# An FNet mixing layer plus a GEGLU layer on one core: the first token tile and the pass borders in a new order, a pool of their own for tiles that transfers empty, the sums of a and b made earlier, and adding transfers into the output

## Chip, cores and metric

The kernel runs on one core of a Trainium2 chip. The metric is the device time of one execution in microseconds (us). The kernel before took 836.38 us, the median of three runs (831.19 to 836.46).

## What is computed

```python
xn = layernorm(x)                                   # x: 2048 tokens x 512, fp32
a = einsum("sd,ed->se", xn, dft_hid_re)             # 512 x 512 matrices
b = einsum("sd,ed->se", xn, dft_hid_im)
y = einsum("ts,se->te", dft_seq_re, a) - einsum("ts,se->te", dft_seq_im, b)   # 2048 x 2048
h = gelu(xn @ w_gate) * (xn @ w_up)                 # 512 -> 1792
out = x + y + h @ w_down
```

## The kernel before, in words

**Arithmetic.** Every fp32 operand of TensorE is split in two: ACT writes the rounded high part (`split_hi`, line 67), DVE subtracts it for the low part (`split_lo`, line 70). A product (`mm3`, line 81) is three multiplications of 128 x 512: high by high, and the two mixed ones. Each large product is made as seven block products (numbered 0 to 6) of sums and differences of blocks; DVE makes the sums. So PE waits for low parts (psl, wl, xT..l) on DVE and for high parts (psh, wh, xT..h) on ACT. All engines work through their instructions in the order in which the program issues them (`manual_schedule`).

**First stage.** Eight token tiles of 128 tokens (`TILES`, t0 to t7) are loaded, normalized, transposed on PE (tile pt), copied (xq), split into xT0 to xT6, and multiplied with the 512 x 512 matrices (d, split into wph and wpl); `plain_out` sends the results to the DRAM tensor ab, which holds a and b for each of the 16 token tiles.

**Units.** 28 units (`unit`, 14 for each half of the tokens; NP is 14). A unit makes the seven products for gate (even) or up (odd) into the PSUM tiles a, b, c; the ACT copies from a and b (lines 568, 575, 580) stand between them. Its other work (weight splits, sums, splits of h) stands in a list with costs (`background`), worked off at four places of the unit by `run(share)`; what is left is put into `carry` for the next unit. Down projections (`down`, PSUM tiles dn) fill in between: ACT copies dn into a tile part, and POOL issues a transfer that adds it to the DRAM tensor partial (lines 443 to 447). In units 4 to 11 DVE also normalizes the transposed second half of x (`norm_xr`).

**Spectral stage.** Between unit 13 and 14 a and b of the second token half are made by seven products in PSUM tiles sa and sb (`spectral`, `prepare`), and go to ab.

**Passes.** Four passes of 16 steps (`steps`) contract over the 16 token tiles. Pass 0 and 1 make, for the two column halves, the products 0, 6, 2; pass 2 and 3 make 5, 4, 3, 1. A step takes three (or four) panels of the sequence matrices (pan, 256 KB each, loaded by SP), sums them on DVE (`sum_step`), splits them into psh and psl (`split_step`), and multiplies with a0, s34 (pass 0, 1) or with b (bth, btl) and qr (qrhl) of the token tile (`contract`). In pass 0 each step also loads a and b of a tile (`load_ab`), makes four half-tile sums of them on DVE (`side_sums`: w34 and qr) and splits some (`side_split`); b is loaded again by SP and split with qr in pass 1 (`late_side`). The PSUM banks of a pass are first filled from partial by ACT (`seed`, line 693). At the end of a pass `drain` empties them: in pass 0 and 1 into tiles tot, from which six transfers add to partial, and, after subtracting from the residual x (xres), into the DRAM tensor ends by four plain transfers; in pass 2 and 3 into the output.

**Memory and queues.** Almost every 128 x 512 tile comes from one pool `mem` of 67 slots (`slot`), pairs of tiles from `big` (21). A tile that a transfer empties (part, tot, xres, ab, xr) sits in its slot until that transfer has landed; who gets the slot next waits for it. SP issues the plain loads in program order, POOL the stores to ab, partial and ends.

Of the kernel before, what the change touches and what calls it, by code (L numbers as in the profile page):

```python
# [27 lines left out]
BIG = 21  # L28
SLOTS = 67
# [5 lines left out]
def fnet_geglu_kernel(ctx: ExitStack, tc: tile.TileContext, x, xt, cs, dh, wgu, wd, out):  # L35
# [8 lines left out]
    mem = ctx.enter_context(tc.tile_pool(name="mem", bufs=SLOTS))  # L44
    small = ctx.enter_context(tc.tile_pool(name="small", bufs=4))
# [4 lines left out]
    def slot(name, dtype=F32, shape=(P, D)):  # L50
        return mem.tile(list(shape), dtype, name=name, tag="mem")

# [41 lines left out]
    ends = dram.tile([2, 2, 2, P, CH], F32, name="ends")  # L94
    ab = dram.tile([NS, 2, P, D], F32, name="ab")
    xnt = dram.tile([2, ND, P, CH], F32, name="xnt")
# [120 lines left out]
    def plain_out(n, m):  # L217
        t = slot("ab")
        nc.scalar.activation(t, xps.pop((n, m)), AF.Copy, scale=-1.0 if m else 1.0)
        to_ab(n, m, t)  # L220
# [7 lines left out]
    def spectral(sp, k, i):  # L228
# [9 lines left out]
        elif k == 1:  # L238
            t = slot("a")
            nc.scalar.activation(t, sa[i], AF.Copy)  # L240
            to_ab(n, 0, t)
        elif k == 5:
            s5[i] = slot("s5")
            nc.scalar.activation(s5[i], sb[i], AF.Copy)
        elif k == 6:
            s6[i] = slot("s6")
# [3 lines left out]
        elif k == 3:  # L250
            t = slot("b")
            nc.scalar.activation(t, sb[i], AF.Copy, scale=-1.0)
            to_ab(n, 1, t)
        elif k == 2:
            nc.vector.tensor_add(s5[i], sa[i], s5[i])
            to_ab(n + TPC, 0, s5[i])
# [24 lines left out]
    def norm_xr(h, t, j):  # L281
        v = xr[h, t, j]
        nc.vector.tensor_sub(v, v, xst[t, 0])
        nc.vector.tensor_mul(v, v, xst[t, 1])
        nc.gpsimd.dma_start(xnt[t, 2 * h + j], v)
# [51 lines left out]
    def prepare(k):  # L337
        for j in range(2):
            sum_x(k, j)
            sum_w(k, j)  # L340
            split(*x1_split(k, j))
# [91 lines left out]
    def down(qs, r, js):  # L433
# [6 lines left out]
        def add():  # L440
            for j in js:
                t = slot("part")
# [7 lines left out]
    SPLIT_AHEAD, SUM_AHEAD, LOAD_AHEAD = 1, 2, 3  # L450
# [8 lines left out]

    FILL = {0: 2, 1: 2, 2: 2, 3: 2, 4: 2, 5: 1}  # L460

    def background(n):
        work = []

# [23 lines left out]
        else:  # L488
            for k in range(4):
# [8 lines left out]
        if n == 2 * NP - 2:  # L498
            put(sum_step, 0)
            put(side_sums, 0, cost=4)  # L500
            put(side_split, 0, cost=3)
        if n == 2 * NP - 1:
            put(split_step, 0, cost=6)
            put(sum_step, 1)
            put(side_sums, 1, cost=4)
# [5 lines left out]
    def unit(n):  # L511
# [4 lines left out]
        if n == 2 * NP - 3:  # L516
            load_ab(0)
            load_step(0)
        if n == 2 * NP - 2:
            for r in GROUP[0]:  # L520
                load_acc(0, r)
            load_ab(1)
            load_step(1)
        if n == 2 * NP - 1:
            load_step(2)
            load_ab(2)
# [42 lines left out]
        multiply(4, c, True)  # L569
        while carry:  # L570
# [19 lines left out]
        if n == 0:  # L590
            add_w(1)
            split_w(1)
        run(.75)
# [3 lines left out]
        d3()  # L597
        high(n, (1, 1))
        low(n, (0, 0))
        nc.vector.tensor_add(q6, c, q6)  # L600
        if n % 2 == 1:
# [6 lines left out]
    GROUP = {0: (0, 6, 2), 1: (5, 4, 3, 1)}  # L608
    passes = [(0, 0), (1, 0), (0, 1), (1, 1)]
    steps = [(c, g, n) for c, g in passes for n in range(NS)]  # L610
    pan, pan_src, pan_hl = {}, {}, {}

# [20 lines left out]
    def split_step(i):  # L633
        if i < len(steps):
            src = pan_src.pop(i)
            for r in GROUP[steps[i][1]]:
                pan_hl[i, r] = hl_tile("ps")
# [4 lines left out]
    def load_ab(n):  # L642
        if n < NS:
            t = pair("abr", F32)
            for m, v in enumerate((av, bv)):
                v[n] = t[:, m]
                nc.sync.dma_start(v[n], ab[n, m])

    def load_b(n):
        bv[n] = slot("b")  # L650
        nc.sync.dma_start(bv[n], ab[n, 1])

    def side_sums(n):
        if n < NS:
            v, w = qr[n], w34[n] = slot("qr"), slot("w34")
            ah, bh = ([t[:, :HD], t[:, HD:]] for t in (av[n], bv.pop(n)))
            nc.vector.tensor_sub(w[:, :HD], ah[0], ah[1])
            nc.vector.tensor_sub(v[:, :HD], bh[1], ah[1])
            neg_sub(v[:, HD:], v[:, :HD], ah[0])
            neg_sub(w[:, HD:], v[:, HD:], bh[0])  # L660

    def side_split(n):
        if n < NS:
            t = pair("s34")
            a0[n], s34[n] = hl_half("a0"), (t[:, 0], t[:, 1])
            split(a0[n], av.pop(n)[:, :HD])
            split(s34[n], w34.pop(n))

# [13 lines left out]
    acc, bank, late = {}, {}, {}  # L682

    def load_acc(c, r):
        t = pair("acc", F32)
        for j in range(2):
            acc[c, r, j] = t[:, j]
            nc.sync.dma_start(acc[c, r, j], partial[c, r, j])
# [6 lines left out]
    def load_residual(c):  # L695
        for h in range(2):
            for j in range(2):
                late[c, h, j] = slot("xres")
                nc.sync.dma_start(late[c, h, j], xt[c, 1, 2 * h + j])

    def load_ends(c):
        for h in range(2):
            for j in range(2):
                late[c, h, j] = slot("ends")
                nc.sync.dma_start(late[c, h, j], ends[c, h, j])

    def store(c, h, j, t, src):
        nc.sync.dma_start(out[2 * h + j, 2 * c + t], src)
# [3 lines left out]
    def drain(c, r, j):  # L712
        ps = bank.pop((c, r, j))
        if r in (0, 6):
            t = slot("tot")
            nc.scalar.activation(t, ps, AF.Copy)
            for u in (5, 1) if r == 0 else (3,):
                nc.gpsimd.dma_start(partial[c, u, j], t, accum_op=OP.add)  # L718
        if r in (6, 2):
            t = late.pop((c, int(r == 6), j))  # L720
            nc.vector.tensor_sub(t, ps, t)
            nc.gpsimd.dma_start(ends[c, int(r == 6), j], t)
        if r == 5:
            us[j] = slot("u")
            nc.scalar.activation(us[j], ps, AF.Copy)
        if r == 4:
            v = slot("v")
            nc.vector.tensor_add(v, ps, us[j])
            for h in range(2):
                t = late.pop((c, h, j))  # L730
                neg_sub(t, v, t)
# [230 lines left out]
```

## Time and profile before

| what | value |
| --- | --- |
| median of three runs | 836.38 us (831.19 to 836.46) |
| the profiled execution's own time | 834.16 us |
| its span, first to last instruction | 832.3 us |
| mean granted TensorE clock | 0.993 |
| PE, DVE, ACT, POOL busy | 97%, 83%, 61%, 16% of the span |
| transfers | 170.65 MB, mean 205 GB/s |

| stretch (us from the span's start) | what runs |
| --- | --- |
| 0 to 55 | first stage |
| 55 to 246 | units 0 to 13 |
| 246 to 286 | spectral stage |
| 286 to 489 | units 14 to 27 |
| 489 to 578 | pass 0 |
| 578 to 650 | pass 1 |
| 650 to 740 | pass 2 |
| 740 to 832 | pass 3 |

How to read it: a row of the timeline has start and duration in us, engine, line, operation, output and inputs, shape and count, and in brackets the idle time of that engine just before and what ended it. `<-DMA partial<-tot` means that a transfer's landing ended the wait. "issue" means that the profile shows nothing that was waited for. A row of the table by stretches has, for each engine, busy us and the number of instructions, then the granted clock, the share of time for which the 16 DMA engines were busy, and GB/s. Some records of multiplications are missing (3514 are there).

### The profile page before, as it was taken

What the parts mean: (1) busy time and instruction counts of PE and PEld (TensorE: products, weight loads), DVE (VectorE), ACT (ScalarE), POOL (GpSimd) and SP (SyncE); (2) the same over time, 40 slices, a digit from 0 to 9 for tenths busy, and PEclk for the clock granted to TensorE, in tenths of its full rate; (3) what the DMA queues carried; (4) which work ended last, traced back from release to release, by engine and by line L of the source; (5) the groups of instructions that cost most, each with busy time, mean ns of one, the idle gap of its engine ahead of it and who ended that gap; (6) DMA issues with size and microseconds to landing.
All of it is one profiled execution on the core that took longest, in us unless ns stands there. A gap on an engine that the chain in (4) does not pass through costs nothing.

```text
span 832.3 us, 11558 instructions
## 1 busy us (share of the span) xinstructions
PE 808.4 (97%) x3514; PEld 656.6 (79%) x3514; DVE 693.5 (83%) x1292; ACT 509.2 (61%) x976; POOL 133.0 (16%) x186
## 2 busy tenths in 40 slices
PE   7999999999999999999999989999899899999998
PEld 4878887788887888888888768788688678887886
DVE  6777999789889758778887979998798699879992
ACT  4566776576686466586666585657566564364441
POOL 0310112222221322132222211112200300000000
PEclk8999999999999999999999999999999999999999
DMA  9722636877891466676577979999998987788732
GB/s 332 274 102 88 184 121 141 198 146 151 238 227 52 177 99 124 133 204 104 109 143 179 230 200 264 278 322 350 317 309 296 318 283 219 236 287 311 252 102 101
DMA packets 88446, 170.65 MB, mean 205 GB/s; under 512 B 10416, under 2 KB 10944, under 8 KB 88256
## 3 DMA queue, kind: packets, MB, share of 16 engines
q1 hardware_dynamic: 67424, 122.46, 44.0%
q0 software_dynamic: 20672, 47.20, 28.1%
q8 instruction: 27, 0.44, 0.2%
q14 instruction: 35, 0.29, 0.1%
q10 hardware_dynamic: 288, 0.26, 0.1%
HBM read 120.59 MB, written 51.39 MB: 207 GB/s over the span
## 4 chain that ended last, share of the span: by engine, by line
PE 43%; issue 31%; DVE 9%; POOL 9%; DMA 5%; ACT 3%; SPq 0%; POOLq 0%; DVEq 0%; ACTq 0%
PE m L81 29%; POOL partial L447 6%; PE b L81 3%; PE dn L81 3%; PE xp L81 3%; PE a L81 2%; DMA partial<-part 2%; DVE psl L70 2%; PE c L81 2%; PE sa L81 1%; DMA partial<-tot 1%; POOL partial L445 1%; POOL partial L718 1%; DMA acc<-partial 1%; DMA pan<-in_cs 1%
## 5 line engine op out<-in xcount | busy, mean ns | idle before, releaser
L67 ACT ACTIVATE psh<-pan 128x512 fp32r<-128x512 f32 x224 | 127.2, 623 | 94.9 <-PE m L81 40.7
L70 DVE TENSOR_TENSOR psl<-pan,psh 128x512 fp32r<-128x512 f32 x224 | 141.1, 685 | 14.1 <-DMA partial<-tot 7.5
L447 POOL DMA_DIRECT2D partial<-part x92 | 80.1, 883 | 264.7 <-ACT part L443 255.4
L443 ACT ACTIVATE part<-dn 128x512 f32<-128x512 f32 x112 | 66.4, 603 | 37.3 <-PE dn L81 30.3
L81 PE MATMUL m<-psh,s 128*128 128x512 f32 x256 | 84.9, 393 | 0.0
L81 PE MATMUL m<-psh,qrhl 128*128 128x512 f32 x256 | 84.2, 390 | 0.5 <-ACT psh L67 0.5
L70 DVE TENSOR_TENSOR wl<-ws,wh 128x512 fp32r<-128x512 f32 x84 | 55.3, 685 | 2.3 <-ACT wh L67 1.6
L81 PEld LDWEIGHTS m<-psh,s 128*128 128x128 f32 x256 | 48.7, 190 | 10.2
L81 PEld LDWEIGHTS m<-psh,qrhl 128*128 128x128 f32 x256 | 48.0, 188 | 10.7 <-ACT psh L67 0.9
L81 PE MATMUL m<-psl,qrhl 128*128 128x512 f32 x128 | 50.5, 395 | 2.4 <-DVE psl L70 2.4
L81 PE MATMUL m<-psl,s 128*128 128x512 f32 x128 | 50.4, 394 | 1.4 <-DVE psl L70 1.4
L67 ACT ACTIVATE wh<-ws 128x512 fp32r<-128x512 f32 x84 | 49.6, 628 | 1.6 <-DMA partial<-part 1.6
L81 PE MATMUL m<-psh,bth 128*128 128x512 f32 x128 | 49.9, 390 | 0.0
L81 PE MATMUL m<-psh,btl 128*128 128x512 f32 x128 | 49.8, 389 | 0.0
L81 PE MATMUL m<-psl,bth 128*128 128x512 f32 x128 | 49.8, 389 | 0.0
L81 PE MATMUL m<-psh,a 128*128 128x512 f32 x128 | 45.4, 395 | 3.5 <-ACT psh L67 1.4
L583 DVE TENSOR_TENSOR w<-c,w 128x512 f32<-128x512 f32 x28 | 19.4, 691 | 34.5 <-ACT w L580 34.2
L580 ACT ACTIVATE w<-b 128x512 f32<-128x512 f32 x28 | 16.7, 597 | 39.6 <-PE b L81 38.3
L81 PE MATMUL b<-xT3h,w 128*128 128x512 f32 x112 | 39.3, 392 | 1.2 <-ACT w L580 1.2
L70 DVE TENSOR_TENSOR wl<-wx,wh 128x512 fp32r<-128x512 f32 x28 | 19.2, 687 | 24.8 <-ACT wh L67 19.6
L70 DVE TENSOR_TENSOR htl<-s,hth 128x512 fp32r<-128x512 f32 x56 | 36.1, 686 | 4.5 <-ACT hth L67 4.1
L422 DVE TENSOR_TENSOR s<-s 128x512 f32<-128x512 f32 x56 | 37.4, 688 | 0.9
(275 smaller groups left out, 2181.1 us busy)
## 6 DMA issues: line engine op xcount, KB each, us to landing
pan<-in_cs SPq DMA_DIRECT2D x224, 256.0 KB, 4.4
partial<-part POOLq DMA_DIRECT2D x112, 256.0 KB, 4.5
wx<-in_wgu SPq DMA_DIRECT2D x56, 256.0 KB, 3.9
abr<-ab SPq DMA_DIRECT2D x32, 256.0 KB, 5.6
wd<-in_wd SPq DMA_DIRECT2D x28, 256.0 KB, 3.0
acc<-partial SPq DMA_DIRECT2D x28, 256.0 KB, 6.0
d<-in_dh SPq DMA_DIRECT2D x16, 256.0 KB, 6.1
ab<-ab POOLq DMA_DIRECT2D x16, 256.0 KB, 2.4
```

The costliest lines, as they stand in the source:

```text
L67: nc.scalar.activation(t[0], src, AF.Copy)
L70: nc.vector.tensor_sub(t[1], src, t[0].bitcast(F32))
L81: nc.tensor.matmul(ps, a[u][:, sl], b[v], start=first and r == 0, stop=last and r == 2, skip_group_check=resumed)
L422: nc.vector.tensor_sub(t, u, v)
L443: nc.scalar.activation(t, ps[j], AF.Copy)
L445: nc.gpsimd.dma_start(partial[sp, r, j], t)
L447: nc.gpsimd.dma_start(partial[sp, r, j], t, accum_op=OP.add)
L580: nc.scalar.activation(w, b, AF.Copy)
L583: nc.vector.tensor_add(w, c, w)
L718: nc.gpsimd.dma_start(partial[c, u, j], t, accum_op=OP.add)
```

## The change

It has five parts. The counts of PE's instructions stay the same.

1. First token tile: its high part is split before ACT turns to the second tile; the tile is normalized by one DVE instruction instead of ACT; the matrices are loaded ahead of the third tile, and both products of t0 come before the transposition of t1. For the later tiles ACT's copy xq comes ahead of DVE's low part.
2. A pool `ship` of nine tiles for what transfers empty (ab, a, b, s5, s6, xn, part, tot, neg, u, v, o, and the new sums); `mem` shrinks to 60 slots, `big` to 20.
3. The sums of a and b are made in the units (unit 1 and 14 to 26, one or two tiles each) and stored to a new DRAM tensor sd. Pass 0 loads half of a and one tile of sd instead of a and b; pass 1 loads b and the other tile of sd, both issued by POOL (`load_late`), two steps ahead of use.
4. Pass borders: seeds for products 2 and 6 of pass 0 are made inside unit 27, product 0 isn't seeded (DVE adds its partial sum at the drain); the loads of partial (acc) are issued by POOL; panels are loaded, summed and, from step 3 of pass 0 to the end of pass 1, split one step further ahead; splits and sums at a border are placed between its products. In the spectral stage sums and splits are spread over its four blocks.
5. The residual goes into the output by eight DRAM-to-DRAM copies in the first stage, and the drains add to it by transfers (`out_y`, four per pass in pass 0 and 1, eight in pass 2 and 3 together); the tensor ends with its loads and subtractions is gone.

```diff
+    def ship(name):
+        return out_pool.tile([P, D], F32, name=name, tag="ship")
...
     def norm_xr(h, t, j):
         v = xr[h, t, j]
         nc.vector.tensor_sub(v, v, xst[t, 0])
-        nc.vector.tensor_mul(v, v, xst[t, 1])
-        nc.gpsimd.dma_start(xnt[t, 2 * h + j], v)
+        w = ship("xn")
+        nc.vector.tensor_mul(w, v, xst[t, 1])
+        nc.gpsimd.dma_start(xnt[t, 2 * h + j], w)
...
+    SIDE_UNITS = (1,) + tuple(range(NP, 2 * NP - 1)) + (NP + 2, NP + 4)
...
+        for k in SIDE_AT.get(n, ()):
+            for f in side_sums(k):
+                put(f, cost=1)
...
+        if n == 2 * NP - 1:
+            seed(0, SEEDED[0][0])
...
+    def split_upto(i):
+        return max(i + 1, min(i + 2, 2 * NS)) if i > 2 else i + 1
...
+    def side_sums(n):
+        v, w = ship("qr"), ship("w34")
...
+            for m, t in enumerate((w, v)):
+                nc.gpsimd.dma_start(sd[n, m], t)
...
+    def load_late(n):
+        if n < NS:
+            bv[n], qr[n] = slot("b"), slot("qr")
+            nc.gpsimd.dma_start(bv[n], ab[n, 1])
+            nc.gpsimd.dma_start(qr[n], sd[n, 1])
...
     def drain(c, r, j):
         ps = bank.pop((c, r, j))
         if r in (0, 6):
-            t = slot("tot")
-            nc.scalar.activation(t, ps, AF.Copy)
+            t = ship("tot")
+            if r == 0:
+                nc.vector.tensor_add(t, ps, acc.pop((c, r, j)))
+            else:
+                nc.scalar.activation(t, ps, AF.Copy)
             for u in (5, 1) if r == 0 else (3,):
                 nc.gpsimd.dma_start(partial[c, u, j], t, accum_op=OP.add)
         if r in (6, 2):
-            t = late.pop((c, int(r == 6), j))
-            nc.vector.tensor_sub(t, ps, t)
-            nc.gpsimd.dma_start(ends[c, int(r == 6), j], t)
+            t = ship("neg")
+            if r == 6:
+                nc.vector.tensor_scalar_mul(t, ps, -1.0)
+            else:
+                nc.scalar.activation(t, ps, AF.Copy, scale=-1.0)
+            nc.gpsimd.dma_start(out[2 * int(r == 6) + j, 2 * c + 1], t, accum_op=OP.add)
...
         if r == 4:
-            v = slot("v")
-            nc.vector.tensor_add(v, ps, us[j])
+            v = ship("v")
+            neg_sub(v, ps, us[j])
             for h in range(2):
-                t = late.pop((c, h, j))
-                neg_sub(t, v, t)
-                store(c, h, j, 1, t)
+                nc.gpsimd.dma_start(out[2 * h + j, 2 * c + 1], v, accum_op=OP.add)
...
+    nc.vector.tensor_scalar(xs[t0], xs[t0], stats[:, 0, 0:1], scale[:, 0, 0:1], op0=OP.subtract, op1=OP.mult)
...
+                nc.gpsimd.dma_start(out[2 * h + j, 2 * sp + 1], xt[sp, 1, 2 * h + j])
...
+    late_at = {NS + 2 + k: k for k in range(NS - 4)}
+    late_at.update({2 * NS + 2 * k: NS - 4 + k for k in range(4)})
...
+        if i + 2 in late_at:
+            load_late(late_at[i + 2])
```

The first place is ACT at the start. Before (L110 loads half of t0, L121 is the root, L137 the normalization, L67 a high part, L176 the copy xq; x_114 is t0, x_121 t1, d are the matrices):

```order
L110 DMA x_114<-in_x 128x256
L121 ACT_TABLE_LOAD
L121 ACTIVATE w<-stats,eps 128x1
L137 ACTIVATE x_114<-x_114,scale 128x512
L121 ACTIVATE w<-stats,eps 128x1
L67 ACTIVATE wph<-d_119 128x512
L67 ACTIVATE xT0h<-pt 128x2x128
```

Now (lines have moved by five: L126 is the root, L72 a high part):

```order
L115 DMA x_117<-in_x 128x256
L126 ACT_TABLE_LOAD
L126 ACTIVATE w<-stats,eps 128x1
L72 ACTIVATE xT0h<-pt 128x2x128
L72 ACTIVATE xT1h<-pt 128x2x128
L72 ACTIVATE wph<-d_126 128x512
L72 ACTIVATE wph<-d_128 128x512
```

The high part of t0 stands four instructions further ahead: the normalization, the second tile's root and one split no longer stand before it.

The second place is POOL at the border from pass 0 to pass 1. Before:

```order
L447 DMA partial<-part 128x512 x44
L718 DMA partial<-tot 128x512 x5
L722 DMA ends<-xres 128x512
L718 DMA partial<-tot 128x512
L722 DMA ends<-xres 128x512 x3
L718 DMA partial<-tot 128x512 x5
```

Now (L455 adds part, L747 tot to partial, L754 adds to the output, L704 loads b, L705 loads qr):

```order
L455 DMA partial<-part 128x512
L747 DMA partial<-tot 128x512 x5
L754 DMA out_y<-neg 128x512
L747 DMA partial<-tot 128x512
L754 DMA out_y<-neg 128x512 x3
L704 DMA b<-ab 128x512
L705 DMA qr<-sd 128x512
L704 DMA b<-ab 128x512
L705 DMA qr<-sd 128x512
```

Six adding and four plain transfers have become ten adding ones, and the loads of b and qr, which SP issued or which weren't there, now stand behind them.

The third place is ACT at the same border. Before (L716 empties a bank into tot, L693 seeds one):

```order
L716 ACTIVATE tot<-m 128x512 x2
L693 ACTIVATE m<-acc 128x512 x2
L67 ACTIVATE psh<-pan 128x512 x3
L67 ACTIVATE bth<-b 128x512
L67 ACTIVATE qrhl<-qr 128x512
L67 ACTIVATE psh<-pan 128x512 x3
```

Now (L745 and L753 empty banks, L72 makes high parts):

```order
L745 ACTIVATE tot<-m 128x512 x2
L753 ACTIVATE neg<-m 128x512 x2
L72 ACTIVATE psh<-pan 128x512 x9
L72 ACTIVATE bth<-b 128x512
L72 ACTIVATE qrhl<-qr 128x512
L72 ACTIVATE psh<-pan 128x512 x3
```

The first split of b stands behind nine panel splits instead of three. These nine are for steps 18, 19 and 20; the three behind qrhl are for step 21 (pass 1 begins with step 16).

## The prediction on record

> **What bounds the kernel now.** I read the page's head first, then the waits of PE, then the stretches, then the timelines where those waits lie.
>
> ```profile
> span 832.3 us, 11558 instructions
> ...
> PE 808.4 (97%) x3514; PEld 656.6 (79%) x3514; DVE 693.5 (83%) x1292; ACT 509.2 (61%) x976; POOL 133.0 (16%) x186
> ```
>
> PE is the bound and does the same multiplications after the change. So only what is not PE's work can be won: 832.3 less 808.4 is 24 us, and some half-clock time inside the 808. Where that lies, PE's waits say (total us, times, longest):
>
> ```profile
> PE m L81 <- DVE psl L70: 5.5, 5, 2.0
> PE xp L81 <- ACT xT0h L67: 2.3, 1, 2.3
> PE sa L81 <- ACT a L240: 1.9, 1, 1.9
> PE m L81 <- ACT psh L67: 1.8, 2, 1.4
> PE b L81 <- ACT b L568: 1.7, 1, 1.7
> ...
> PE b L81 <- ACT w L580: 1.2, 2, 1.0
> PE m L81 <- ACT m L693: 1.1, 1, 1.1
> PE m L81 <- DVE a L70: 1.0, 1, 1.0
> PE c L81 <- ACT xT4h L67: 0.5, 1, 0.5
> ...
> PE c L81 <- DVE w L583: 0.5, 1, 0.5
> PE dn L81 <- DVE htl L70: 0.3, 1, 0.3
> ```
>
> These are 17.8 us in 18 stops. Each stop also costs about 0.25: the first multiplication behind one has a row of 0.50 where the pipelined ones have 0.39 (below), and the pitch behind it is wider. The stretches (PE, PEld, DVE, ACT, POOL busy; clock; DMA share; GB/s):
>
> ```profile
> 9.28:17.44 8.16, 7.68 (x21) 5.15 (x22) 6.21 (x18) 3.98 (x10) 0.00 (x0) 0.63 1.05 392
> 286.20:489.00 202.80, 201.11 (x887) 166.02 (x885) 155.41 (x294) 132.24 (x258) 46.70 (x58) 1.00 0.69 150
> 589.00:599.25 10.25, 6.48 (x19) 4.54 (x19) 7.69 (x13) 7.01 (x14) 1.68 (x3) 0.83 1.06 334
> 602.00:632.00 30.00, 30.00 (x134) 24.86 (x133) 29.97 (x51) 20.51 (x39) 0.00 (x0) 1.00 0.88 295
> ```
>
> In the units (row 2) PE is full and DVE at 77%. At the border of pass 0 and 1 (row 3) the clock falls to 0.83 over 10.25 us: 1.7 us lost beside the stops.
>
> **The change, part by part**, against the profiled execution's own 834.16 us (2.2 below the median of 836.38, inside the runs' 831.19 to 836.46).
>
> *1. Start.*
>
> ```profile
> 4.28 0.43 DVE L206 CAST wph<-d 128x512 fp32r<-128x512 f32 x1
> 5.03 0.16 DVE L128 SCALAR_TENSOR_TENSOR scale<-w 128x1 f32<-128x1 f32 x1
> 6.33 0.63 PE L151 MATMUL pt<-ident,x 128*128 128x128 f32 x4 [0.51 <-issue]
> 8.87 0.36 ACT L67 ACTIVATE xT0h<-pt 128x256 fp32r<-128x256 f32 x1
> 9.28 0.80 PE L81 MATMUL xp<-wph,xT0h 128*128 128x512 f32 x1 [2.32 <-ACT xT0h L67]
> ```
>
> The transposes of t0 end at 6.96, but its high part starts at 8.87, since ACT has other work ahead. Now: scale ready 5.19; one DVE normalization, priced as the DVE cast of the same size, 0.43; transposes 0.63; high part 0.36; three handovers of some 0.07: first product at 6.8, or −2.5, of which I give back 0.2 because products then wait for t1's columns. −2.3. Bounds: −1.5 if the second matrix is not there before 7.8; −4 if the half-clock time at the start also shrinks. The xT4h stop (0.5) falls to the new order of xq and low parts: −0.5 (0 to −0.75).
>
> The Trainium skill ("TensorE: Matmul & The Clock Gate", Part 1, what the clock gate does) has PE at half rate until about 3.4 us of sustained work. The row 9.28:17.44 has 0.63 over 8.16, a loss of 3.0; by that rule it would be 1.7, and the time 1.3 lower; I keep the row's.
>
> *2. The ship pool.*
>
> ```profile
> 154.71 0.69 DVE L70 TENSOR_TENSOR wl<-wx,wh 128x512 fp32r<-128x512 f32 x1 [4.03 <-DMA partial<-part]
> ...
> 589.78 0.69 DVE L70 TENSOR_TENSOR psl<-pan,psh 128x512 fp32r<-128x512 f32 x1 [3.77 <-DMA partial<-tot]
> ...
> 661.84 1.15 ACT L67 ACTIVATE psh<-pan 128x512 fp32r<-128x512 f32 x2 [7.00 <-DMA partial<-tot]
> ...
> partial<-part POOLq DMA_DIRECT2D x112, 256.0 KB, 4.5
> ...
> b<-ab SPq DMA_DIRECT2D x16, 256.0 KB, 4.3
> ```
>
> Splits stood still because a slot still held a tile that was leaving. With tiles that leave in a pool of their own this wait goes to whoever makes the next such tile. In the units part's transfer lands 4.5 us after issue, and nine tiles cover that; so the ACT w stops (1.2 in 2) go with their 2 × 0.25: −1.7 (bounds 0 and −1.7). The DVE w stop stays.
>
> *3. Sums of a and b in units 14 to 26 and unit 1.*
>
> ```profile
> 568.05 0.42 DVE L657 TENSOR_TENSOR w<-abr 128x256 f32<-128x256 f32 x1
> ...
> 478.13 0.63 ACT L67 ACTIVATE s<-w 128x512 fp32r<-128x512 f32 x1 [3.76 <-DVE w L77]
> ```
>
> Four sums of a tile are 4 × 0.4 = 1.6 us; fifteen tiles from unit 14 on make 24 on 155.4 of 202.8: 179, or 88%. PE sees none of it as long as DVE has room: units 4 to 11 carry two more 128x512 operations each, and show one DVE stop of 0.5. I take +1.0 (two such stops with what follows them); bounds 0 and +16 (thirteen units with 1.25 each). The split that waited at 478.13 held up ACT's copy b (1.7 stop): it moves to unit 27; −1.95 and +0.75 back for unit 27's larger list: −1.2. Pass 0 is relieved of 14 × 1.6 on DVE and half of its loads.
>
> *4. Spectral stage:* sums and splits spread over four blocks; the ACT a stop (1.9) goes: −1.9 (0 to −2.3, with its 0.25).
>
> *5. Start of pass 0:* two products seeded in unit 27, the third added at the drain. The m seed (1.1), DVE a (1.0) and htl (0.3) stops and one psl stop of 0.7 go, with 4 × 0.25 but less 0.2 for a longer drain: −3.9 (−1 to −4.1).
>
> *6. Border of pass 0 and 1.* Two things happen. The slot wait of 3.77 goes. But on POOL ten adding transfers now stand ahead of the loads of b and qr, and ACT's split of b stands ahead of the panel split of step 21 (step 36 at the next border).
>
> ```profile
> 575.64 2.64 POOL L718 DMA_DIRECT2D partial<-tot  x3 [6.60 <-ACT tot L716]
> 582.84 0.88 POOL L718 DMA_DIRECT2D partial<-tot  x1 [4.55 <-issue]
> 584.85 0.87 POOL L718 DMA_DIRECT2D partial<-tot  x1 [1.13 <-issue]
> ...
> 586.88 0.85 POOL L718 DMA_DIRECT2D partial<-tot  x1 [0.59 <-issue]
> ...
> 589.96 1.12 POOL L722 DMA_DIRECT2D ends<-xres  x2 [2.23 <-issue]
> 591.83 0.55 POOL L722 DMA_DIRECT2D ends<-xres  x1 [0.74 <-issue]
> ```
>
> Three adding transfers go out at once, the fourth 7.2 later, then one every d; only three seem to be under way at a time. So the tenth goes out at 7.2 + 6d behind the first, and the loads at 7.2 + 7d. They take 0.3 to issue, 4.5 to land (partial's row; b's has 4.3), and 1.1 goes for the two high parts ahead of the panels: ready at 13.1 + 7d. PE's need:
>
> ```profile
> 534.49 4.08 PE m L81 x18
> ...
> 577.84 0.39 PE L81 MATMUL m<-psh,a 128*128 128x512 f32 x1
> ...
> 590.52 0.50 PE L81 MATMUL m<-psl,s 128*128 128x512 f32 x1 [1.41 <-DVE psl L70]
> 594.80 0.50 PE L81 MATMUL m<-psl,a 128*128 128x512 f32 x1 [0.99 <-DVE psl L70]
> ...
> 665.00 0.50 PE L81 MATMUL m<-psl,qrhl 128*128 128x512 f32 x1 [1.97 <-DVE psl L70]
> ```
>
> Step 16 begins 2.2 behind the first adding transfer; step 21 is five steps of 4.08 later, at 22.6. At the other border steps of 24 products take 5.44, so step 36 is at 2.2 + 4 × 5.44 = 24.0. What is d? Over the rows (591.83 − 582.84) / 4 = 2.25, while panels crowd the DMA engines (1.06); the longest interval is 3.1; three under way with 4.5 each, as in the units, give 1.5. Half of what crowds there (a, b and all panels of the next steps) is lighter after the change, so I take the middle, 1.9: ready at 26.4, PE stops 3.8 and 2.4 us. Border 0/1: before, 1.4 + 1.4 + 1.0 + 3 × 0.25 + 1.7 clock = 6.2; after, 3.8 + 0.25 + 1.7 = 5.75; −0.45. Border 1/2: before, 0.5 + 2.0 + 2 × 0.25 = 2.95; after, 2.65 without a loss of clock (none there before either); −0.3. Border 2/3: one psl stop of 0.4 goes, −0.6.
>
> *At nothing:* norm_xr's other target (same count on DVE); the DRAM copies of the residual, under the first stage's products, whose transfers have nobody waiting at once (ab is first read in unit 1); the drains (DVE has four operations per border before and after, ACT loses the seeds of product 0); the end, where adding transfers precede the last plain store and land inside its time (0 to +3).
>
> **Sum:** −2.3 − 0.5 − 1.7 + 1.0 − 1.2 − 1.9 − 3.9 − 0.6 = −11.1, borders −0.75: −11.85. 834.16 − 11.85 = **822.3 us**.
>
> **Rivals.** Without the two borders the sum is 823.06; each case then adds its borders less the 9.15 of before.
> - *The queue is quick* (d 1.5): ready at 23.6, stops 1.0 and 0. 823.06 + 1.25 − 9.15 = 815.2. For it: the units' 4.5. Against: every interval quoted.
> - *The queue is as slow as before* (d 2.25): ready 28.85, stops 6.25 and 4.85, each with 0.25 and 1.7 of clock: 15.0. 828.9. For it: the rows as they stand.
> - *Slower than before:* d is 3.1, since ten adding transfers alternate with panels. Ready 34.8, stops 12.2 and 10.8, with 2 × 1.95: 26.9, so 840.8. It decides from d of 2.6, where the borders' 20.2 eat all of 11.1. Against: one interval alone was that long.
> - *DVE becomes the bound in the units:* 88% is a mean over units with unequal lists, and some come near to full. 13 × 1.25 = 16.2 in place of 1.0: 837.5. For it: pass 1, full at 29.97 of 30, shows how little is left then. Against: units 4 to 11.
> - *Pass 1 is bound by transfers:* a step loads five tiles, not four: share 0.88 × 5/4 = 1.10, so 12 steps × 4.08 × 0.10 = 4.9, 827.2. Against: 392 GB/s at the start, where 1.31 MB in 4.08 is 321. The Trainium skill ("DMA: Bandwidth & Descriptors", issuing engines are not separate queues) has all issuers share the same sixteen engines, so that POOL as issuer gains no bandwidth; the rows here do not contradict it.
>
> **How the numbers follow.** Forecast 0.42, quick queue 0.22, slow queue 0.18, slower queue 0.06, DVE 0.07, transfers 0.05. The likeliest case's own range is 817 to 827; to hold 8 in 10 it goes down through the quick queue and up through the slow one: 812 to 832. One per cent (8.4 us) is about what a measurement can tell from no change. Below 828.0 lie the forecast, the quick queue, transfers, and less than half of the slow queue: 0.68. Above 844.7 lies the slow tail of the slower queue and of DVE: 0.07. Within: 0.25.
>
> **What would show it.** First product near 6.8. No wait of splits for partial's landing. At both borders one PE stop, at steps 21 and 36, behind ACT's bth and qrhl waiting for their loads; POOL's adding transfers 1.9 apart. DVE near 88% in units 14 to 27, with hardly a PE stop. DMA share under 1 in pass 1. I am wrong if PE stops elsewhere at the borders, if b comes in time, or if units 14 to 26 each show a stop.

## The result and the profile after

The changed kernel took 845.45 us, the median of four runs (843.75 to 848.63), beside 835.71 for four runs of the kernel before: a ratio of 1.0132, with a 95% interval of 1.0085 to 1.018. The forecast was 822.3 with a range of 812 to 832 and a chance of 0.07 for slower by over 1%. The sign was wrong.

The profiled execution's own time is 845.09 us, against 834.16. Its page begins:

```profile
span 843.3 us, 11706 instructions
...
PE 808.4 (96%) x3514; PEld 657.0 (78%) x3514; DVE 690.6 (82%) x1288; ACT 505.9 (60%) x972; POOL 197.6 (23%) x294
```

PE does the same work in the same busy time (half-clock time that the start no longer has comes back at the borders); POOL is busy half as long again. So the 11 us are idle time of PE. To see where, I took the start of the first multiplication of each stage from both timelines of PE and put the forecast's terms beside it:

| stage | before, us | after, us | difference | forecast |
| --- | --- | --- | --- | --- |
| up to unit 0 | 54.79 | 52.66 | -2.13 | -2.3 |
| units 0 to 13 | 191.05 | 188.12 | -2.93 | -2.2 |
| spectral stage | 41.20 | 39.49 | -1.71 | -1.9 |
| units 14 to 27 | 203.13 | 200.62 | -2.51 | -1.55 |
| pass 0 | 87.67 | 85.33 | -2.34 | -2.55 |
| pass 1 | 71.52 | 77.25 | +5.73 | -0.45 |
| pass 2 | 90.91 | 102.34 | +11.43 | -0.3 |
| pass 3, to its last multiplication | 88.02 | 90.17 | +2.15 | -0.6 |
| from there to the end | 4.01 | 7.32 | +3.31 | 0 |

Up to pass 1 the kernel gained 11.6 us where the forecast had 10.5; then it lost 22.6. PE's waits in the new profile (total us, times, longest):

```profile
PE m L86 <- ACT psh L72: 12.5, 2, 8.1
PE m L86 <- DVE psl L75: 7.7, 4, 3.1
PE m L86 <- ACT m L731: 2.2, 3, 0.9
```

All three groups are waits of the passes (m), and 22.4 us together; the largest of the units and the spectral stage is 0.6. They lie at three borders; the end of the kernel is a fourth loss, which no wait of PE shows.

**Border of pass 0 and 1.** POOL's timeline, then ACT's, then PE's:

```profile
564.14 1.77 POOL L747 DMA_DIRECT2D partial<-tot  x2 [2.61 <-DVE tot L743]
567.59 0.88 POOL L747 DMA_DIRECT2D partial<-tot  x1 [1.67 <-DVE neg L751]
571.07 0.87 POOL L747 DMA_DIRECT2D partial<-tot  x1 [2.61 <-issue]
...
585.47 0.86 POOL L754 DMA_DIRECT2D out_y<-neg  x1 [1.41 <-DMA pan<-in_cs]
586.16 0.75 POOL L704 DMA_DIRECT2D b<-ab  x1
588.33 0.58 POOL L705 DMA_DIRECT2D qr<-sd  x1 [1.41 <-DMA pan<-in_cs]
```

```profile
593.12 0.63 ACT L72 ACTIVATE bth<-b 128x512 fp32r<-128x512 f32 x1 [19.78 <-DMA b<-ab]
593.71 0.63 ACT L72 ACTIVATE qrhl<-qr 128x512 fp32r<-128x512 f32 x1
594.24 1.65 ACT L72 ACTIVATE psh<-pan 128x512 fp32r<-128x512 f32 x3
```

```profile
594.91 0.80 PE L86 MATMUL m<-psh,a 128*128 128x512 f32 x1 [8.12 <-ACT psh L72]
```

The fourth to the tenth adding transfer go out in 585.47 - 571.07 = 14.4 us, 2.40 apart; b goes out 22.0 us behind the first and is split 29.0 behind it. ACT stands for 19.8 us at that split, with the panels of step 21 behind it, and PE stops for 8.1. The row of PE names ACT and psh, whose cause is one instruction further back, the bth row's bracket. The stretch around it has a low clock besides:

```profile
584.00:602.00 18.00, 9.24 (x29) 6.78 (x28) 8.22 (x14) 8.88 (x17) 8.64 (x16) 0.72 0.98 305
```

**Border of pass 1 and 2.** The same at step 36, and ahead of it three stops at the seeded banks:

```profile
673.23 0.63 ACT L72 ACTIVATE bth<-b 128x512 fp32r<-128x512 f32 x1 [12.33 <-DMA b<-ab]
```

```profile
675.38 0.80 PE L86 MATMUL m<-psh,qrhl 128*128 128x512 f32 x1 [4.42 <-ACT psh L72]
678.24 0.80 PE L86 MATMUL m<-psl,qrhl 128*128 128x512 f32 x1 [2.07 <-DVE psl L75]
```

```profile
675.00:690.00 15.00, 12.55 (x42) 9.81 (x43) 14.79 (x24) 7.65 (x14) 4.85 (x9) 0.72 0.81 256
```

Here too the clock is low behind the stops: from 678.24 to 683.10 PE's multiplications start 0.44 us apart where they have 0.23 at full clock, eleven times, which is 2.3 us more. The stops at the seeded banks begin with this row of ACT:

```profile
645.27 1.20 ACT L731 ACTIVATE m<-acc 128x512 f32<-128x512 f32 x2 [5.42 <-DVE tot L743]
```

**Border of pass 2 and 3.** SP's timeline and the DVE row that waits for its load:

```profile
744.69 1.02 SPq L734 DMA_DIRECT2D out_y<-u  x2
747.31 2.04 SPq L734 DMA_DIRECT2D out_y<-o  x2
749.40 25.90 SPq L644 DMA_DIRECT2D pan<-in_cs  x25
```

```profile
757.34 0.69 DVE L654 TENSOR_TENSOR pan<-pan 128x512 f32<-128x512 f32 x1 [3.43 <-DMA pan<-in_cs]
```

SP's next panels stand behind the four stores, which wait for the drains. In the kernel before a stop of 0.4 was left here; now it is 3.1. But the panels stood behind stores there too:

```profile
744.38 25.54 SPq L618 DMA_DIRECT2D pan<-in_cs  x31
```

```profile
748.61 0.69 DVE L628 TENSOR_TENSOR pan<-pan 128x512 f32<-128x512 f32 x1 [0.58 <-DMA pan<-in_cs]
```

SP went back to panels 4.1 us behind the first multiplication of pass 3 (744.38 - 740.27), and does so at 3.6 now (749.40 - 745.81). From there to DVE's sum it took 4.2 us and takes 7.9 now. New beside these panels are the four adding transfers of product 4, which land 6.5 us after issue; SP's stores land 4.5 and 6.3 after issue (medians of u and o), where those of o took 2.6 before.

**The end.** POOL's last transfers, and the DMA view of 820 to 845 (busy share in tenths and GB/s, 40 slices of 0.63 us):

```profile
830.76 2.65 POOL L762 DMA_DIRECT2D out_y<-v  x3 [81.98 <-DVE v L82]
835.05 0.86 POOL L762 DMA_DIRECT2D out_y<-v  x1 [1.64 <-issue]
```

```profile
DMA  0000000000000000000949979999999999100000
GB/s 0 0 0 0 0 0 0 0 0 0 0 0 0 0 0 0 0 0 0 52 75 203 138 128 246 256 226 213 236 370 233 259 316 349 56 0 0 0 0 0
```

The same view of the kernel before:

```profile
DMA  0000001991999994830000000000000000000000
GB/s 0 0 0 0 0 0 59 380 380 46 380 390 370 380 387 174 303 120 0 0 0 0 0 0 0 0 0 0 0 0 0 0 0 0 0 0 0 0 0 0
```

Here no panel is loaded in either. With plain stores the busy engines move 380 GB/s; beside four adding transfers they are just as busy and move 200 to 260 in most slices. The last plain store lands 4.9 us after its issue (before 1.9).

### The profile page after: what moved, and what is told of

Same layout as the page of the kernel before. It is cut to its first block, busy times and chain, and to the rows that moved or that the text cites. A ratio compares the mean times of both kernels' runs of the same rounds, so it can differ in the third digit from the quotient of the medians.

```text
span 843.3 us, 11706 instructions
## 1 busy us (share of the span) xinstructions
PE 808.4 (96%) x3514; PEld 657.0 (78%) x3514; DVE 690.6 (82%) x1288; ACT 505.9 (60%) x972; POOL 197.6 (23%) x294
## 4 chain that ended last, share of the span: by engine, by line
PE 80%; DVE 6%; DMA 5%; issue 4%; POOL 2%; ACT 2%; SPq 0%; DVEq 0%; POOLq 0%; ACTq 0%
PE m L86 30%; PE dn L86 14%; PE b L86 11%; PE a L86 8%; PE c L86 8%; PE xp L86 5%; PE sb L86 2%; DMA pan<-in_cs 2%; DMA b<-ab 2%; PE sa L86 1%; POOL partial L747 1%; DMA xraw<-xnt 1%; DVE ws L369 1%; DMA acc<-partial 1%; POOL out_y L754 1%
## 5 line engine op out<-in xcount | busy, mean ns | idle before, releaser
L72 ACT ACTIVATE psh<-pan 128x512 fp32r<-128x512 f32 x212 | 120.7, 622 | 99.5 <-PE m L86 57.3
L75 DVE TENSOR_TENSOR psl<-pan,psh 128x512 fp32r<-128x512 f32 x212 | 134.3, 684 | 17.4 <-ACT psh L72 14.0
L455 POOL DMA_DIRECT2D partial<-part x92 | 80.8, 891 | 194.1 <-ACT part L451 177.1
L86 PE MATMUL m<-psh,qrhl 128*128 128x512 f32 x256 | 86.2, 398 | 5.4 <-ACT psh L72 4.4
L86 PE MATMUL m<-psh,s 128*128 128x512 f32 x224 | 74.3, 394 | 0.0
L72 ACT ACTIVATE wh<-ws 128x512 fp32r<-128x512 f32 x84 | 49.6, 629 | 2.1 <-PE dn L86 2.1
L86 PEld LDWEIGHTS m<-psh,s 128*128 128x128 f32 x224 | 42.8, 191 | 9.0
L86 PE MATMUL m<-psh,a 128*128 128x512 f32 x112 | 40.0, 399 | 8.1 <-ACT psh L72 8.1
L86 PE MATMUL m<-psl,s 128*128 128x512 f32 x112 | 44.1, 393 | 0.0
L762 POOL DMA_DIRECT2D out_y<-v x8 | 7.1, 1089 | 148.0 <-DVE v L82 145.0
```

Source lines behind the costliest of these rows:

```text
L72: nc.scalar.activation(t[0], src, AF.Copy)
L75: nc.vector.tensor_sub(t[1], src, t[0].bitcast(F32))
L86: nc.tensor.matmul(ps, a[u][:, sl], b[v], start=first and r == 0, stop=last and r == 2, skip_group_check=resumed)
L455: nc.gpsimd.dma_start(partial[sp, r, j], t, accum_op=OP.add)
L762: nc.gpsimd.dma_start(out[2 * h + j, 2 * c + 1], v, accum_op=OP.add)
```

## Experiments

Two theories stood against each other at the borders: that POOL's queue makes b late (few transfers under way, or the place behind them), and that the DMA engines are full there, so that order and number change nothing. The ratios of each group are to runs of the kernel before on the same chip, so kernels of different groups are compared by ratios. One table for what the theories turn on; PE needs the first split of b about 21.5 us behind the first adding transfer (22.6 less the two high parts):

| kernel | first split of b behind the first adding transfer | stop at step 21 | ratio to before |
| --- | --- | --- | --- |
| the change | 593.12 - 564.14 = 29.0 | 8.1 | 1.0132 |
| more descriptor space | 592.39 - 565.36 = 27.0 | 6.4 | 1.0046 |
| one panel instead of three | 588.63 - 563.91 = 24.7 | 3.9 | 1.0058 |
| both of these | 585.50 - 564.48 = 21.0 | 0.3 | (one run) |
| neg by plain stores | 588.28 - 564.26 = 24.0 | 3.4 | 0.9992 |
| b and qr five steps ahead | 576.95 - 567.87 = 9.1 | none | 0.9973 |
| b and qr loaded by SP | 572.87 - 563.77 = 9.1 | none | 0.9959 |

**1. More descriptor space.**

```diff
-dynamic_dma_scratch_size=1024
+dynamic_dma_scratch_size=2048
```

> The changed kernel with one number changed: the space for POOL's transfer descriptors is 2048 bytes instead of 1024. Theory A (the queue): POOL can have only three adding transfers under way because that space is full with three; with six, the ten of a border go out faster (interval about 1.2 us instead of 2.4), the loads of b and qr behind them are ready before steps 21 and 36, the stops of 8.1 us and of 4.4 and 2.1 us vanish with their half-clock time, about 20 us in all, and the fourth adding transfer at the end goes out at once (about 3 us): 822 to 826 us. Theory B (the DMA engines): their share is 0.98 at the border, so the transfers end no sooner however many are under way: 840 or more, stops of the same length.

Measured: 838.60 us, ratio 1.0046 (1.0027 to 1.0065), 0.86 points under the change. POOL's timeline and ACT's:

```profile
565.36 4.47 POOL L747 DMA_DIRECT2D partial<-tot  x5 [2.50 <-DVE tot L743]
568.65 2.06 POOL L754 DMA_DIRECT2D out_y<-neg  x1
569.20 2.40 POOL L747 DMA_DIRECT2D partial<-tot  x1
...
578.47 0.58 POOL L704 DMA_DIRECT2D b<-ab  x1 [1.15 <-PE m L86]
```

```profile
592.39 0.63 ACT L72 ACTIVATE bth<-b 128x512 fp32r<-128x512 f32 x1 [17.71 <-DMA b<-ab]
```

Neither theory had it. The space does set how many are under way: seven transfers go out one right behind the other instead of three, and b goes out 13.1 us behind the first instead of 22.0. But it is split only 2.0 sooner, because the landings are still 2.1 apart and each transfer now takes 14 to 15 us. So the engines' pace, not the room, set most of d at this border. At the next one, where SP's panels take less of the engines (29.2% of their time in 645 to 660, against 46.4% in 564 to 592), the same edit took the two stops of step 36, 6.5 us together, to one of under 1 us. The Trainium skill ("DMA: Bandwidth & Descriptors", SWDGE vs HWDGE vs iDMA) says that GpSimd writes its descriptors into rings in a part of SBUF that is set aside. The section gives no number of transfers under way for a given space; that the number rises with the space here fits what it says.

**2. SP loads b and qr.**

```diff
-            nc.gpsimd.dma_start(bv[n], ab[n, 1])
-            nc.gpsimd.dma_start(qr[n], sd[n, 1])
+            nc.sync.dma_start(bv[n], ab[n, 1])
+            nc.sync.dma_start(qr[n], sd[n, 1])
```

> The changed kernel, but SP instead of POOL issues the loads of b and qr for pass 1 and the beginning of pass 2. Theory A (the queue): the loads no longer stand behind the adding transfers; the stops at steps 21 and 36 vanish, about 20 us: 823 to 829 us; POOL's adding transfers keep their interval of about 2.4 us, since nobody waits for them. Theory B (the DMA engines are full there): b comes as late as before, or the panels behind it on SP do; the stops move or stay: 838 or more. With five loads of 256 KB per step on SP pass 1 could also show short stops of its own, some 5 us.

Measured: 831.61 us, ratio 0.9959 (0.9943 to 0.9975). Both stops behind b are gone, as theory A had it, and with them 14.5 us of the expected 20; with the same transfers, what changed is the queue that they stand in. In their place pass 1 shows one stop behind a late panel. SP's panels and the adding transfers still share the engines: from 575 to 593 POOL's queue has 55.2% of their time and SP's 53.8%, and a panel lands 9.3 us after its issue.

```profile
593.48 0.80 PE L86 MATMUL m<-psl,a 128*128 128x512 f32 x1 [2.77 <-DVE psl L75]
```

**3. The last output tiles by DVE and SP.** Pass 3 loads the four tiles of the output in step 11, and:

```diff
-                nc.gpsimd.dma_start(out[2 * h + j, 2 * c + 1], v, accum_op=OP.add)
+                nc.vector.tensor_add(res[h, j], v, res[h, j])
+                nc.sync.dma_start(out[2 * h + j, 2 * c + 1], res[h, j])
```

> The changed kernel, but in pass 3 the four tiles of the output that product 4 completes are loaded by SP in step 11, added on DVE and stored by SP, instead of being added by POOL. If the tail is the fourth adding transfer, which goes out only when the first has landed, the time from the last multiplication to the end falls from 7.3 to about 4 us: 842 us. Rival: four more operations of 0.69 on DVE at the end delay the last drains, and half of that comes back: 844.

Measured: 843.33 us, ratio 1.0096 (1.0068 to 1.0123). From the last multiplication (837.01) to the end (841.2) it is 4.2 us instead of 7.3. The first theory had the size right, but not the reason: with descriptor space of 2048 the fourth transfer went out at once, and the end still took 7.5 us (830.18 to 837.7). It is the plain stores beside the adding ones that land late: the last one takes 4.9 us in the changed kernel, and without adding transfers beside it 1.9 in the kernel before.

**4. POOL stores at the end of pass 2.**

```diff
-        nc.sync.dma_start(out[2 * h + j, 2 * c], src)
+        (nc.sync if c else nc.gpsimd).dma_start(out[2 * h + j, 2 * c], src)
```

> The changed kernel, but POOL instead of SP issues the four plain stores into the output at the end of pass 2. If the stop of 3.1 us at the beginning of pass 3 comes from SP waiting for the drains with the panels behind them in its queue, it falls to about 0.4: 842.5 us. Rival: the panels wait for slots and not for the stores: no change, 845.5.

Measured: 840.37 us, ratio 1.0065 (1.0048 to 1.0082). SP's timeline of 736 to 760 is one unbroken row of panels, and the stop at the beginning of pass 3 is gone:

```profile
736.08 21.96 SPq L644 DMA_DIRECT2D pan<-in_cs  x19
```

So panels issued ahead of the stores remove the stop. That the place behind the stores alone made it grow is not shown: before, the place was the same. The gain is 5.6 us by the ratios, more than the stop. Part of it is no work of this edit: in this profile the first stop of step 36, which lies ahead of the edited stores, is 1.9 us instead of 4.4 (2.9 in experiment 3).

**5. Edits 2, 3 and 4 together.**

> The changed kernel with three edits together: SP issues the late loads of b and qr, pass 3 loads, adds and stores the last four output tiles by DVE and SP, POOL issues the four plain stores at the end of pass 2. If the three losses are separate, their gains against the change (14.5, 3.0 and 5.6 by the ratios of the single runs) add up to 23, less 1.6 because the queues' stores at the end of pass 2 are no longer followed by a second stop: 822 to 826 us, that is 1.0 to 1.5% faster than before. If the later stops only collected what the earlier ones had left, the sum is smaller: 829 or more.

Measured: 823.29 us, ratio 0.9858 (0.9822 to 0.9894). That is the expected sum: the three losses are separate and add up, as far as the ratios can tell.

**6. POOL loads b and qr five steps ahead.**

```diff
-        if i + 2 in late_at:
-            load_late(late_at[i + 2])
+        if i + 5 in late_at:
+            load_late(late_at[i + 5])
```

> The changed kernel, with POOL still issuing the loads of b and qr, but five steps ahead of use instead of two, so that the first three tiles stand ahead of the border's ten adding transfers. Theory Q (place in the queue): only the place behind the adding transfers made them late; the stops at steps 21 and 36 go, and with a stop of about 3 us left from panels that compete with the adding transfers, as when SP issued the loads, the time is 830 to 834. Theory E (the engines are full, the order does not matter): what is loaded earlier pushes the adding transfers and the panels back, and the stops stay above 5 us: 839 or more.

Measured: 832.73 us, ratio 0.9973 (0.9954 to 0.9991). The loads stay on POOL, only ahead of the adding transfers, and the stops at steps 21 and 36 are gone: what held b back was its place in the queue. Stops behind low parts of panels stay, 9.0 us in five (changed kernel 7.7 in four).

**7. One panel instead of three in steps 19 to 26.**

```diff
-            for m, t in ((0, 0), (0, 1), (1, 1), (1, 0))[:3 + g]:
+            for m, t in ((0, 0), (0, 1), (1, 1), (1, 0))[:1 if NS + 3 <= i < NS + 11 else 3 + g]:
...
+            if NS + 3 <= i < NS + 11:
+                pan_src[i] = {0: c0, 6: c0, 2: c0}
```

> The changed kernel, but steps 19 to 26 load one panel instead of three and use it for all three products, without the sum (what it computes is changed). Theory E (adding transfers and panels share the engines' time): with panels gone, three adding transfers under way go at their undisturbed pace, 4 to 4.5 us each, so 1.5 us apart instead of 2.4; the loads are ready 20 us behind the first one, and the stop at step 21 of 8.1 us goes: 832 to 834. Theory R (POOL's queue is slow by itself, three at a time at 7 us each): 2.3 us apart, stop of 7 us or more: 843 or more.

Measured: 839.55 us, ratio 1.0058 (1.0033 to 1.0084), between the two. Without most of the panels the adding transfers go out 2.04 us apart (568.95 to 581.19 for six) instead of 2.40: the panels that are left out account for 0.36 of d, not for 0.9.

**8. The same with descriptor space of 2048.**

> The same with descriptor space of 2048 bytes. Theory E: an adding transfer takes the engines 1.3 us without panels, so the landings of the ten are 1.3 us apart and the loads of b and qr ready some 16 us behind the first. Theory R: the landings are 2.0 us apart as with panels.

Measured in one run: 828.04 us. The ten land between 568.83 and 584.57 in the trace, 1.75 apart; theory E had 1.3 and theory R 2.0. With all panels and the same space (experiment 1) it was 2.1, so the panels are worth about as much here as in experiment 7. The first split of b is 21.0 us behind the first transfer, and PE stops for 0.3. The DMA view of 569 to 593 (0.6 us a slice):

```profile
DMA  9999999899999999999999999999999999999999
GB/s 178 171 198 154 109 191 229 191 242 263 246 277 222 208 201 212 201 222 191 212 195 225 331 403 399 410 427 417 379 365 413 382 406 362 410 376 396 369 348 376
```

This is the plainest view of the price. Up to about 582 POOL's adding transfers have the engines nearly to themselves: POOL's queue has 96.8% of the engines' time from 569 to 582, SP's 13.5% with overlap, and the engines are full at some 200 GB/s. When the plain loads of b and qr follow in the same queue, the same engines, as full, move 400. Plain tiles land some 0.67 us apart there, adding ones 1.75, which is 2.6 times as much.

**9. neg by plain stores.**

```diff
-            nc.gpsimd.dma_start(out[2 * int(r == 6) + j, 2 * c + 1], t, accum_op=OP.add)
+            nc.gpsimd.dma_start(ends[c, int(r == 6), j], t)
```

> The changed kernel, but the four transfers per border that add neg into the output are plain stores into a tensor of their own, at the same place in POOL's queue (the output lacks them). Theory E (an adding transfer costs the engines about 1.75 us, a plain one 0.67): the queue ahead of b shrinks by 4 x (2.4 - 0.7 to 1.0), 5.6 to 6.8 us per border; the stop at step 21 falls from 8.1 to about 2, the ones at step 36 (4.4 and 2.1) to under 3 together, with less half-clock time: 833 to 837. Theory L (what counts is the latency of whatever stands in the queue, and a plain store is as slow there, as the loads' landing of 6.9 behind the adding ones suggests): stop above 5 us, 841 or more.

Measured: 833.80 us, ratio 0.9992 (0.9968 to 1.0016). As theory E had it, though with less at step 21: b is split 5.0 us sooner, the stop falls to 3.4 (expected about 2), and the two of step 36 vanish. So it costs about 12 us by the ratios that these eight transfers add into the output instead of being plain stores.

**10. Edits 2, 3, 4 and descriptor space of 2048.**

> The three edits together (late loads on SP, last output tiles by DVE and SP, four stores on POOL) and descriptor space of 2048 bytes. If, with the loads out of POOL's queue, nobody waits for the adding transfers, more of them under way change nothing: 822 to 825, as with the three edits alone. If more adding transfers at once take the engines from the panels of steps 17 to 22, the stops in pass 1 grow: 826 or more.

Measured: 824.38 us, ratio 0.9885 (0.9852 to 0.9919): no gain over 823.29, as the first reading had it. Once nobody waits in that queue, its depth is worth nothing. Pass 1 has one stop behind a late panel of 3.7 us, where experiment 5 has five of 0.3 to 0.6; but with 1024, too, experiments 2 and 11 have one of 2.8 and 2.6, so the depth need not be its cause.

**11. Edits 2, 3, 4, and the panels of step 32 split one step later.**

```diff
-        return max(i + 1, min(i + 2, 2 * NS)) if i > 2 else i + 1
+        return max(i + 1, min(i + 2, 2 * NS - 1)) if i > 2 else i + 1
```

> The three edits together, and the panels of step 32 are split inside the last step of pass 1 instead of one step earlier. Theory S: PE's three stops for seeded banks at this border (1.8, 1.0 and 0.6 with the wider pitch) come from DVE, where the drain of product 0 stands behind the four low parts of step 32; with these behind the drains the three stops vanish, and PE waits at most 1 us for the first low part: 820 to 822 against 823.3. Rival: drain and seeding take 2.4 us per product and PE 1.36, so the stops stay, and the low parts come later still: 823 to 826.

Measured: 819.63 us, ratio 0.9815 (0.9779 to 0.985), the fastest of all kernels here. The interval overlaps with that of experiment 5, so the 3.6 us between the two by the ratios are not resolved by them alone; the trace shows what the edit did. DVE's timeline now has the drains ahead of the four low parts, and PE's waits for seeded banks, 2.8 us in experiment 5, are gone from its list; instead it waits 1.1 us for the first parts of step 32:

```profile
633.50 1.28 DVE L743 TENSOR_TENSOR tot<-m,acc 128x512 f32<-128x512 f32 x2
635.97 1.29 DVE L751 TENSOR_SCALAR neg<-m 128x512 f32<-128x512 f32 x2 [1.19 <-ACT tot L745]
637.17 2.49 DVE L75 TENSOR_TENSOR psl<-pan,psh 128x512 fp32r<-128x512 f32 x4
```

## Why the prediction was wrong

**Right: everything before pass 1.** The terms for the start, the units, the spectral stage and pass 0 gave 10.5 us, and the traces show 11.6. Two of them came out otherwise than given. At the start:

```profile
6.37 0.63 PE L156 MATMUL pt<-ident,x 128*128 128x128 f32 x4 [1.02 <-DVE x L805]
7.47 0.50 PE L86 MATMUL xp<-wph,xT0h 128*128 128x512 f32 x1 [0.47 <-ACT xT0h L72]
```

```profile
9.28:17.44 8.16, 6.95 (x26) 4.09 (x26) 6.06 (x16) 4.44 (x10) 2.31 (x5) 1.00 1.05 390
```

The first product starts at 7.47 and not at 6.8, and PE then waits in short stops for low parts of the matrices; but the half-clock time is gone (clock 1.00 in the stretch that had 0.63), which the forecast had kept as a bound only. Both together give the forecast's size, which is luck as far as the start goes.

In the units the sums cost nothing, where the forecast took 1.0 and gave 0.07 to DVE as the bound:

```profile
286.20:489.00 202.80, 202.36 (x890) 166.51 (x889) 180.24 (x357) 139.43 (x272) 64.46 (x90) 1.00 0.86 220
```

DVE is at 180 of 202.8, as worked out (179), and PE at 202.4. An engine at 89% beside a full one still hid its work.

**Wrong, the size of d (step 6).** The mechanism was the one forecast: ten adding transfers, the loads behind them, ACT's split behind the loads, a stop at steps 21 and 36. The formula held in its sum: ready at 13.1 + 7d, with the measured 2.40, is 29.9, and the panels of step 21 were split 30.1 us behind the first transfer. In that two errors cancel: b went out 22.0 us behind the first transfer and not 24.0, and its split began 7.0 us later and not 4.8. What failed is "half of what crowds there is lighter after the change, so I take the middle, 1.9". The rows said 2.25 (it counts the five moments at which an adding transfer's landing made room; plain stores went out beside them). The trace showed no cause for it, and I took crowding by panels for the cause and discounted it. What crowds did get lighter: from the first adding transfer on SP's queue has 46.2% of the engines' time (564 to 592) where it had 55.5% (576 to 592), and d grew all the same. The runs show that panels are worth 0.36 of it (experiment 7), and that an adding transfer occupies the engines 1.75 us even where few panels compete and seven are under way (experiment 8). The lower bound of 1.5, from transfers in the units, was a latency of 4.5 divided by three, where 102 of the 112 go out with at most one other under way; it was no pace that the queue had shown. With 2.40 the sum of the rivals, which has 1.7 of clock at both borders, gives 17.1 for the borders and 831.0, near the rival of the slow queue. So d alone does not explain 845.

**Wrong, what was dropped at the border of pass 1 and 2 (step 6).** The forecast put 2.65 in the place of the 2.95 us of stops there, as if the new stop took the old ones' place. It came on top: a psl stop of 2.0 is still there, at 660.00 where 665.00 stood. Before, DVE's low part waited for a slot; now it waits for nothing, but six sums and two splits of b and qr stand ahead of it on DVE, which works without a pause from 651.53 on. First before, then now:

```profile
664.25 1.29 DVE L70 TENSOR_TENSOR psl<-pan,psh 128x512 fp32r<-128x512 f32 x2 [3.71 <-DMA partial<-tot]
```

```profile
657.21 0.68 DVE L654 TENSOR_TENSOR pan<-pan 128x512 f32<-128x512 f32 x1
...
659.26 2.49 DVE L75 TENSOR_TENSOR psl<-pan,psh 128x512 fp32r<-128x512 f32 x4
```

So the slot wait went, as forecast, and the change's own order on DVE made a stop of the same size; this is read from the rows, no run tests it. And three stops for seeded banks are new, 2.2 us, 2.7 with the pitch. DVE's drain of product 0 stands behind the low parts of step 32; experiment 11 shows that this made them. The forecast counted the drains ("DVE has four operations per border before and after") and did not look at what they stand behind. Last, the stop at step 36 was priced "without a loss of clock (none there before either)", though the rivals have 1.7 for it; it cost 2.3.

**Wrong, the border of pass 2 and 3 (step 6).** "One psl stop of 0.4 goes, -0.6"; it grew to 3.1. SP and the adding transfers were named nowhere there: SP's panels stand behind stores that wait for drains, as before, and now land later beside four adding transfers. Experiment 4 shows that panels ahead of the stores do away with the stop; how much of its growth is the company and how much the place stays open.

**Wrong, the end (at nothing).** 0 with a bound of +3; measured +3.3. That the adding transfers precede the last plain store was so, and it was no excuse: the store shares the engines with them (experiment 3, and the end of experiment 1).

**The rivals.** The slower rival was this mechanism at d = 3.1; it was right about the sign with a d that did not occur, so by luck. The other losses did the rest of the 14 us from 831.0 to 845.1: 2.7 for the seeded banks, 2.2 for the psl stop that stayed, 2.8 at the border of pass 2 and 3, 3.3 at the end, and about 4 because the stops of steps 21 and 36 (8.1 + 0.6 and 4.4 + 2.1, where the sum has 7.3 and 5.9) and the half-clock time behind them were longer; the stages up to pass 0 gave back 1.1. The rival of pass 1 bound by transfers did show once b was in time: with SP as issuer there is a stop of 2.8 us behind a late panel (experiment 2).

What stays open: why an adding transfer takes 1.3 us in some intervals (837.45 to 838.82 at the end) and 2.0 in others. The runs give the mean, not the cause.

## What to carry to other kernels

An adding transfer is priced by the engine time that it takes, not by its landing: look for stretches where the engines are full and GB/s falls to half. Put a load that somebody waits for ahead of such transfers in its queue, or in another queue, and count every store that stands ahead of the next stage's loads. Where an old stop is struck from the sum because its wait goes, look at what the change puts ahead of the same instruction on its own engine, and keep a new stop beside the old ones until a row shows that they have the same cause.

## What the runs showed of the hardware

- Adding transfers of 256 KB landed 1.75 us apart with the engines nearly to themselves and seven under way, 2.1 beside panels; plain ones 0.67. Full engines moved some 200 GB/s with the one and 400 with the other.
- With descriptor space of 1024 three adding transfers are under way, with 2048 six or seven; beside panels that doubled each one's time (from about 7 to 15 us) and moved the last landing little.
- PE kept its full clock at the start where the pause between the transposes and the first product shrank from 2.3 to 0.5 us; before, it ran at 0.63 for the next 8 us. There the granted clock was still 1.00 from 7.0 to 8.0 and 0.50 from 8.6 on, with PE idle since 6.96.
